# Zero products at the start, a norm turned on VectorE through DRAM, and new list priorities in a transformer layer

## The chip, the cores and the metric

One core of one Trainium2 chip runs the kernel. The metric is the device time of one execution in microseconds (us); the time given for a kernel is the median of several runs. The engines are called PE (TensorE, matmuls), ACT (ScalarE), DVE (VectorE), POOL (GpSimd) and SP (SyncE, which issues the DMAs here).

## The reference

A transformer layer on one sequence of S = 2048 rows and D = 640 columns, float32: layer norm, attention over eight keys at distances 0, 2, ..., 14, a residual, layer norm, a SwiGLU FFN with F = 1728, a residual. 32 heads of 20 columns.

```python
def _A_ref(x, wqkv, wo):
    qkv = (x @ wqkv).reshape(B, S, 3, H, Dh) ...
    off = jnp.arange(W) * dil            # W = 8, dil = 2
    idx = pos[:, None] - off[None, :]
    ...
    logits = jnp.einsum("bhsd,bhswd->bhsw", q, kg) * scale
    logits = jnp.where(mask[None, None, :, :], logits, -1e9)
    attn = _softmax(logits, axis=-1)
    o = jnp.einsum("bhsw,bhswd->bhsd", attn, vg)
    return o.transpose(0, 2, 1, 3).reshape(B, S, D) @ wo

def _B_ref(x, w_gate, w_up, w_down):
    return (_silu(x @ w_gate) * (x @ w_up)) @ w_down

h = x + _A_ref(_layernorm(x), A_wqkv, A_wo)
h2 = h + _B_ref(_layernorm(h), B_w_gate, B_w_up, B_w_down)
```

## The kernel before, in words

**Blocks.** The rows are cut into NB = 4 blocks of 512. A block lies on 128 partitions as NJ = 4 row tiles j of 640 columns. D is cut into NC = 5 chunks of 128.

**Products in three passes.** Every matmul operand is split into a high half, rounded to the type fp32r, and a low half, the remainder. A product is the sum of high x high, high x low and low x high. ACT makes the high half by a cast, DVE the low half by a subtraction. So each weight and each activation costs one ACT and one DVE instruction before PE may use both halves.

**First norm (ln1).** Rows are centred into the buffer XN; the factor 1/std is left for the eviction of the product (L405), so the products need only the centred rows. PE turns them into columns, four 128x128 transposes for each of five groups (x_columns, to_columns; L313), ACT casts them (L316), DVE subtracts (L317). Block 0 does so row tile by row tile (L361, L363, L364), with DVE computing the statistics of its first three tiles (L273 to L275). Blocks 0 and 2 go into the tile sha, blocks 1 and 3 into shb.

**Query, key, value (qkv, L400).** NG = 4 head groups of 8 heads; for each block, group and row tile 15 matmuls 128x480. Weights of a group are loaded in five pieces (load_wqkv; L374 and L376 split them). The results go to DRAM (ksc, vsc, qsc).

**Attention (att_load, att_qk, att_exp, att_av).** It runs on DVE, in 16 units of a block and a group, as long elementwise instructions and reductions (L448, L453, L479, L487; the first two take 2.8 us each), and ends with a turn (L494) and stores to osc.

**Output projection (wo, L569), residual, second norm, columns (ln2_columns).** wo(0) runs among the last qkv products, wo(b + 1) among the products of block b's FFN. Block 3 (TURN) makes its columns without PE: DVE turns 32x32 squares in place (L716), four transfers store them to xsc and one loads them back so that a chunk of columns lies on each partition (ln2_turn, L718 and L722); ACT and DVE then split them out of XN (L711, L712).

**FFN (ffn).** NF = 14 tiles of 128 columns of F. For each tile a gate and an up product into PSUM banks 5 and 6 (proj, L630: three passes of five matmuls for each bank), silu on ACT (L661), product on DVE (L662), split (L663, L665), and the down product of the tile before (down, L642), which accumulates in banks 0 to 4. Then finish adds the residual and stores (L681 to L700).

**The order of the work.** Nothing is issued in program order. Every step is first recorded with an engine, an estimated cost, the regions that it reads and writes, and a priority (Plan.add). Plan.order then runs a list scheduler over all engines: when an engine falls free, the ready operation with the lowest priority number goes next, and the list that results is the order in which each engine gets its instructions. SP transfers are given a modelled bus time and a latency (LAT, LAT0). PR holds the priorities. Products have priority 10, attention on DVE 20. One look-ahead rule exists: an operation of priority 20 or more waits if one of priority 1 would become ready before it ends. The list is fixed when the kernel is built; on the chip an engine waits for whatever its next instruction needs.

## Time and profile before

| | us |
|---|---|
| median of 3 runs | 869.96 (869.52 to 870.01) |
| the profiled execution | 870.27 |
| its span, first to last instruction | 868.5 |
| PE busy | 855.7 (99%) |
| DVE busy | 641.7 (74%) |
| ACT busy | 401.4 (46%) |
| POOL busy | 1.6 |

A row of the groups reads: line, engine, operation, tiles out<-in, shape, count, then busy time in us, mean ns of one, idle time of the engine just before them and what ended it. A row of the waits reads: engine and tile, line, what was waited for, then us in total, times, longest. A row of the windows reads: stretch, length, busy time of PE, weight loads (PEld), DVE, ACT and POOL with their counts, then the granted clock of PE, the DMA share and GB/s. The timeline merges neighbouring instructions of one line: start, length, engine, line, shape, count. The chain of waits is followed back from the last instruction; its rows are start, length, what. Matmuls are pipelined, so the time of a run of them divided by their number is the time that one costs, not the length of a single one.

### The profile page before, as it was taken

What the parts mean: (1) busy time and instruction counts of PE and PEld (TensorE: products, weight loads), DVE (VectorE), ACT (ScalarE), POOL (GpSimd) and SP (SyncE); (2) the same over time, 40 slices, a digit from 0 to 9 for tenths busy, and PEclk for the clock granted to TensorE, in tenths of its full rate; (3) what the DMA queues carried; (4) which work ended last, traced back from release to release, by engine and by line L of the source; (5) the groups of instructions that cost most, each with busy time, mean ns of one, the idle gap of its engine ahead of it and who ended that gap; (6) DMA issues with size and microseconds to landing.
All of it is one profiled execution on the core that took longest, in us unless ns stands there. A gap on an engine that the chain in (4) does not pass through costs nothing.

```text
span 868.5 us, 10718 instructions
## 1 busy us (share of the span) xinstructions
PE 855.7 (99%) x4036; PEld 726.8 (84%) x4036; DVE 641.7 (74%) x743; ACT 401.4 (46%) x651; POOL 1.6 (0%) x7
## 2 busy tenths in 40 slices
PE   6999999999999999999999999999999999999998
PEld 5888888889978888888888888878988888888886
DVE  6489699999999999999999999995212116333332
ACT  5857732223682434574443567443464334333321
POOL 0000000000000000000000000000000000000000
PEclk9999999999999999999999999999999999999999
DMA  7995764596887969659997986887437645322201
GB/s 252 272 292 162 202 174 133 155 289 173 296 243 236 295 227 272 191 158 305 363 300 237 304 228 194 237 304 244 141 124 246 243 148 181 107 91 91 97 26 61
DMA packets 74612, 180.11 MB, mean 207 GB/s; under 512 B 28720, under 2 KB 39344, under 8 KB 73792
## 3 DMA queue, kind: packets, MB, share of 16 engines
q1 hardware_dynamic: 74560, 179.43, 65.6%
q8 instruction: 31, 0.51, 0.3%
q14 instruction: 21, 0.17, 0.1%
HBM read 138.36 MB, written 41.03 MB: 207 GB/s over the span
## 4 chain that ended last, share of the span: by engine, by line
PE 77%; DVE 18%; issue 2%; DMA 2%; SPq 0%; ACT 0%; DVEq 0%
PE bank L630 32%; PE bank L400 23%; PE bank L642 16%; PE bank L569 5%; DVE fa L487 3%; DVE fa L479 3%; DVE fa L448 3%; DVE fa L453 3%; PE bank L313 1%; DVE acts L665 1%; DVE fa L662 1%; DMA osc<-fa 1%; DVE fa L494 1%; DVE shb L317 1%; DMA fa<-in_x_dram 1%
## 5 line engine op out<-in xcount | busy, mean ns | idle before, releaser
L630 PE MATMUL bank<-shb,ra 128*128 128x512 f32 x1620 | 381.2, 390 | 2.3 <-DVE shb L317 2.1
L630 PEld LDWEIGHTS bank<-shb,ra 128*128 128x128 f32 x1620 | 303.1, 188 | 66.2 <-DVE shb L317 3.3
L642 PE MATMUL bank<-ra,acts 128*128 128x512 f32 x656 | 160.3, 391 | 0.0
L642 PEld LDWEIGHTS bank<-ra,acts 128*128 128x128 f32 x656 | 122.5, 188 | 25.1
L662 DVE TENSOR_TENSOR fa<-bank,fa 128x512 f32<-128x512 f32 x52 | 35.7, 687 | 129.2 <-PE bank L630 128.9
L400 PE MATMUL bank<-ra,sha 128*128 128x480 f32 x480 | 108.4, 385 | 0.0
L400 PE MATMUL bank<-ra,shb 128*128 128x480 f32 x470 | 104.7, 380 | 0.0
L400 PEld LDWEIGHTS bank<-ra,sha 128*128 128x128 f32 x480 | 91.4, 192 | 13.7
L607 ACT CAST ra<-fa 128x1280 fp32r<-128x1280 f32 (+1 forms) x56 | 68.8, 1229 | 66.4 <-PE bank L630 64.7
L400 PEld LDWEIGHTS bank<-ra,shb 128*128 128x128 f32 x470 | 87.5, 188 | 12.8
L479 DVE TENSOR_TENSOR fa<-fa 128x1280 f32<-128x1280 f32 x64 | 93.7, 1487 | 1.0
L448 DVE TENSOR_TENSOR fa<-fa 128x2560 f32<-128x2560 f32 x32 | 90.3, 2821 | 2.6 <-DMA fa<-qsc 2.1
L487 DVE TENSOR_TENSOR fa<-fa 128x1280 f32<-128x1280 f32 (+2 forms) x96 | 89.7, 935 | 2.7
L453 DVE TENSOR_REDUCE fa<-fa 128x128 f32<-128x2560 f32 x32 | 90.1, 2815 | 0.6
L405 ACT ACTIVATE st<-bank,fa 128x480 f32<-128x480 f32 x64 | 42.0, 658 | 84.8 <-PE bank L400 82.0
L661 ACT ACTIVATE fa<-bank 128x512 f32<-128x512 f32 x52 | 31.1, 598 | 107.7 <-PE bank L630 107.6
L624 DVE TENSOR_TENSOR ra<-fa,ra 128x640 fp32r<-128x640 f32 (+1 forms) x82 | 64.7, 817 | 16.2 <-ACT ra L608 14.0
L569 PE MATMUL bank<-ra 128*128 128x320 f32 x480 | 74.5, 309 | 0.0
L569 PEld LDWEIGHTS bank<-ra 128*128 128x128 f32 x480 | 72.4, 188 | 2.1
L608 ACT CAST ra<-fa 128x640 fp32r<-128x640 f32 x56 | 40.7, 728 | 63.0 <-PE bank L642 62.8
L663 ACT CAST acts<-fa 128x512 fp32r<-128x512 f32 x52 | 32.3, 621 | 49.5 <-DVE fa L662 49.4
L642 PE MATMUL bank<-acts,ra 128*128 128x512 f32 x164 | 46.3, 390 | 0.1
(82 smaller groups left out, 486.1 us busy)
## 6 DMA issues: line engine op xcount, KB each, us to landing
fa<-in_ffn_dram SPq DMA_DIRECT2D x52, 960.0 KB, 6.0
ra<-lsc SPq DMA_DIRECT2D x26, 640.0 KB, 5.4
fa<-ksc SPq DMA_DIRECT2D x32, 440.0 KB, 5.8
fa<-vsc SPq DMA_DIRECT2D x32, 440.0 KB, 5.8
ra<-lsc SPq DMA_DIRECT2D x30, 320.0 KB, 3.7
lsc<-ra SPq DMA_DIRECT2D x13, 640.0 KB, 5.1
ksc<-st SPq DMA_DIRECT2D x32, 160.0 KB, 4.4
qsc<-st SPq DMA_DIRECT2D x16, 320.0 KB, 3.5
```

Source lines behind the costliest of these rows:

```text
L400: T.matmul(banks[bk][:, 0:480], l, r_(wq(g, w, c), 480), start=(p, c) == first_mm, stop=(p, c) == last_mm)
L405: P.add("ACT", act(480) + 0.06, lambda bk=bk, j=j: A.activation(stage_t()[:, so : so + 1920].rearrange("p (t j c) -> p t j c", t=3, j=NJ)[ ...
L448: P.add("DVE", dve(2560), lambda: V.tensor_tensor(f(PROD, 2560).rearrange("p (j w c) -> p j w c", j=2, w=W), window(ko, 2 * jp), f(qo + 32 ...
L453: P.add("DVE", dve(2560), lambda: V.tensor_reduce(f(lo + 128 * jp, 128), f(PROD, 2560).rearrange("p (n d) -> p n d", d=DH), axis=AX.X, op= ...
L479: V.tensor_tensor(f(PROD + 1280 * jj, 1280).rearrange("p (w h d) -> p w h d", w=W, d=DH), f(vo + 160 * j, 1280).rearrange("p (w h d) -> p ...
L487: V.tensor_add(dst(v), v[:, :, 0:m, :], v[:, :, m : 2 * m, :])
L569: T.matmul(banks[bk][:, 0:320], l, r_(m, 320), start=p == 0 and c == 0, stop=p == 2 and c == NC - 1)
L607: P.add("ACT", act(n), lambda: A.copy(r_(gu, n), f(raw, n)), r=[rf(raw, n)], w=[rr(gu, n)], prio=PR["fh"])
L624: P.add(eng, c, lambda o=o: E.tensor_sub(ra[p0:, lo + o : lo + o + 640], fa[p0:, raw + o : raw + o + 640], ra[p0:, hi + o : hi + o + 640]. ...
L630: T.matmul(banks[bk], r_(gu + 1280 * w + wid * c + col, 128), x2(a, c), start=p == 0 and c == 0, stop=p == 2 and c == NC - 1)
L642: T.matmul(banks[k], l, m, start=first and p == 0, stop=last and p == len(passes) - 1)
L662: P.add("DVE", dve(512), lambda so=so: V.tensor_mul(f(so, 512), banks[6], f(so, 512)), r=[pb(6), rf(so, 512)], w=[rf(so, 512)], prio=0)
```

## The change

Five things change.

1. POOL clears 128 columns of the weight tile (WARM). PE multiplies them with themselves 20 times ahead of everything else, into bank 4, and three times more behind the transposes of block 0's first row tile. The results are overwritten.
2. Block 3's first norm (TURN1) is turned as its second one was: ACT centres the rows into XN sorted for DVE's turn, using the source as scratch space; one DVE turn of 2560 columns, four stores to a new DRAM tile ysc, one load, then five casts on ACT and five subtractions on DVE out of XN. The 20 PE transposes of that norm are gone. The code of ln2_turn becomes turn_rows and serves both norms.
3. In the first FFN tile of each block the up product's pass high x high comes before the gate product's second pass. Other tiles keep their order.
4. The look-ahead rule takes priorities up to 1 instead of exactly 1, and PE holds a product back for at most 0.3 us if an operation with wo(0)'s priority is about to be ready.
5. 19 of the 22 priorities in PR have other values (x, ost and fl stay), and there is a new one for the stores of item 2.

```diff
+TURN1 = (3,)
-PR = {'x': 6, 'wqd': 2.5, 'wqh': 3, 'wql': 2.5, 'qev': 1, 'kvs': 3, 'atl': 3, 'exp': 8, 'ost': 0.5, 'wod': 6, 'woh': 3, 'wol': 2, 'old': 1, 'fld': 3, 'lst': 3, 'wev': 1, 'fh': 2, 'fl': 8, 'ln1': 6, 't1': 2, 'wo0': 1.5, 'wo': 2}
+PR = {'x': 6, 'yst': 1, 'wqd': 8, 'wqh': 2.2, 'wql': 2.2, 'qev': 0.5, 'kvs': 6, 'atl': 2.2, 'exp': 1.2, 'ost': 0.5, 'wod': 1.5, 'woh': 0.9, 'wol': 1.5, 'old': 0.9, 'fld': 1, 'lst': 6, 'wev': 1.5, 'fh': 1.2, 'fl': 8, 'ln1': 3, 't1': 4, 'wo0': 0.4, 'wo': 4}
...
             prio, n = ready[e][0]
+            if e == "PE" and prio >= 10:
+                soon = min((a for a, m in pend[e] if ops[m][4] == PR["wo0"]), default=1e9)
+                if soon < t + 0.3:
+                    free[e] = soon
+                    continue
             if prio >= 20:
-                soon = min((a for a, m in pend[e] if ops[m][4] == 1), default=1e9)
+                soon = min((a for a, m in pend[e] if ops[m][4] <= 1), default=1e9)
                 if soon < t + ops[n][1] - 0.3:
                     free[e] = soon
                     continue
...
+                inplace = self.center and self.turned
...
+                if inplace:
+                    def rows():
+                        A.activation(src(j), src(j), AF.Identity, accum_out=f(SUM, 1))
+                        A.mul(f(NEG, 1), f(SUM, 1), -1.0 / D)
+                        A.activation(self.sorted_row(j), src(j).rearrange("p (f t) -> p f t", t=32), AF.Identity, bias=f(NEG, 1))
+                    P.add("ACT", 1.95, rows, ..., prio=self.prio)
+                    P.add("ACT", 1.0, lambda: A.activation(src(j), src(j), AF.Square, bias=f(NEG, 1), accum_out=f(SS, 1)), ..., prio=self.prio + 1)
+                    return
...
+        def turn_rows(scratch, key, b, prio, sprio):
+            P.add("DVE", dve(2560), lambda: V.transpose(f(XN, 2560), f(XN, 2560)), ..., prio=prio)
+            for q in range(4):
+                P.add("SP", 0.65, lambda q=q: Q.dma_start(
+                    scratch[b, :, q, :].rearrange("(f c) t -> c f t", c=32),
+                    fa[32 * q : 32 * q + 32, XN : XN + 2560].rearrange("p (f t) -> p f t", f=20)), ..., prio=sprio, nbytes=nb(640, 512))
+            P.add("SP", 0.65, lambda: Q.dma_start(f(XN, 2560).rearrange("p (k t) -> p k t", k=NC), scratch[b].rearrange("(k c) q t -> c k (q t)", c=128)), ..., prio=sprio, nbytes=nb(640, 2048))
+
+        def turned_columns(t, nm, prio):
+            for k in range(NC):
...
+                w = lambda a, k=k: [(nm, 2560 * a + 640 * j + 128 * k, 2560 * a + 640 * j + 128 * k + 128) for j in range(NJ)]
+                P.add("ACT", act(512), lambda col=col, src=src: A.copy(col(0), src()), ..., w=w(0), prio=prio)
+                P.add("DVE", dve(512), lambda col=col, src=src: V.tensor_sub(col(1), src(), col(0).bitcast(F32)), ..., w=w(1), prio=prio)
...
+        WARM = XH + 1280
+
+        def warm(n, after=()):
+            def mm():
+                for _ in range(n):
+                    T.matmul(banks[4][:, 0:128], r_(WARM, 128), r_(WARM, 128), start=True, stop=True)
+            P.add("PE", 0.2 * n, mm, r=[rr(WARM, 128), *after], w=[pb(4)], prio=0)
...
+                if b in TURN1:
+                    turn_rows(ysc, "Y", b, PR["ln1"], PR["yst"])
+                    turned_columns(t, nm, PR["t1"])
+                    return
...
             for j in range(NJ):
+                if j == 1:
+                    warm(3, [("b5", 0, 0.25)])
...
-        def proj(bk, gu, col, wid):
+        def proj(bks, gu, wid, first):
+            passes = ((0, 0), (0, 1), (1, 0))
...
+            todo = [(n, p) for n in range(len(bks)) for p in range(3)]
+            if first:
+                todo.insert(1, todo.pop(3))
+            for n, p in todo:
+                w, a = passes[p]
+                P.add("PE", 1.145, lambda ...: mm(bk, 128 * n, p, w, a), ..., w=[pb(bks[n])], prio=10)
...
+        P.add("POOL", 0.3, lambda: G.memset(r_(WARM, 128).bitcast(F32), 0.0), w=[rr(WARM, 128)], prio=0)
         load_x(0, (0,))
+        warm(20)
```

More of the change, by code (lines that the diff above doesn't have):

```diff
@@ L177, in program @@
         xsc = dr.tile([NB, D, 4, 128], F32, name="xsc")
+        ysc = dr.tile([NB, D, 4, 128], F32, name="ysc")
         lsc = dr.tile([NF, 128, 1920], F32, name="lsc")
@@ L251, in one @@
                 SUM, NEG, SS = self.SUM + j, self.NEG + j, self.SS + j
-                junk = (lambda: act_t()[:, 3072:3712]) if self.turned else (lambda: f(xo, 640))
+                inplace = self.center and self.turned
+                junk = (lambda: src(j)) if inplace else (lambda: act_t()[:, 3072:3712]) if self.turned else (lambda: f(xo, 640))
+                if inplace:
[3 more added lines that the diff above has]
+                        A.activation(self.sorted_row(j), src(j).rearrange("p (f t) -> p f t", t=32), AF.Identity, bias=f(NEG, 1))
+                    P.add("ACT", 1.95, rows, r=[self.srcr(j)], w=[self.srcr(j), rf(XN, 2560), rf(SUM, 1), rf(NEG, 1)], prio=self.prio)
+                    P.add("ACT", 1.0, lambda: A.activation(src(j), src(j), AF.Square, bias=f(NEG, 1), accum_out=f(SS, 1)),
+                          r=[self.srcr(j), rf(NEG, 1)], w=[self.srcr(j), rf(SS, 1)], prio=self.prio + 1)
+                    return
                 def s1():
@@ L264, in one, with sorted_row @@
                           r=[rf(xo, 640)], w=[self.srcr(j), rf(SS, 1)], prio=self.prio + 1)
+            def sorted_row(self, j):
+                return f(XN, 2560).rearrange("p (f j t) -> p f j t", j=NJ, t=32)[:, :, j, :]
             def one_dve(self, j):
@@ L300, in apply @@
                 if self.turned:
-                    o = f(XN, 2560).rearrange("p (f j t) -> p f j t", j=NJ, t=32)[:, :, j, :]
+                    o = self.sorted_row(j)
                     i = lambda j: self.src(j).rearrange("p (f t) -> p f t", t=32)
@@ L304, in apply @@
                       r=[self.srcr(j), rf(self.NB + j, 1), rf(self.RS + j, 1)], w=[rf(XN, 2560) if self.turned else rf(xo, 640)], prio=self.prio)
+        def turn_rows(scratch, key, b, prio, sprio):
+            P.add("DVE", dve(2560), lambda: V.transpose(f(XN, 2560), f(XN, 2560)), r=[rf(XN, 2560)], w=[rf(XN, 2560)], prio=prio)
+            for q in range(4):
+                P.add("SP", 0.65, lambda q=q: Q.dma_start(
+                    scratch[b, :, q, :].rearrange("(f c) t -> c f t", c=32),
+                    fa[32 * q : 32 * q + 32, XN : XN + 2560].rearrange("p (f t) -> p f t", f=20)),
+                    r=[rf(XN, 2560)], w=[(f"{key}{b}", q, q + 1)], prio=sprio, nbytes=nb(640, 512))
+            P.add("SP", 0.65, lambda: Q.dma_start(f(XN, 2560).rearrange("p (k t) -> p k t", k=NC), scratch[b].rearrange("(k c) q t -> c k (q t)", c=128)),
+                  r=[(f"{key}{b}", 0, 4)], w=[rf(XN, 2560)], prio=sprio, nbytes=nb(640, 2048))
+        def turned_columns(t, nm, prio):
+            for k in range(NC):
+                col = lambda a, k=k: t()[:, 2560 * a : 2560 * a + 2560].rearrange("p (j c q t) -> p c j q t", j=NJ, c=NC, q=4)[:, k]
+                src = lambda k=k: f(XN + 512 * k, 512).rearrange("p (q j t) -> p j q t", q=4, j=NJ)
+                w = lambda a, k=k: [(nm, 2560 * a + 640 * j + 128 * k, 2560 * a + 640 * j + 128 * k + 128) for j in range(NJ)]
+                P.add("ACT", act(512), lambda col=col, src=src: A.copy(col(0), src()), r=[rf(XN + 512 * k, 512)], w=w(0), prio=prio)
+                P.add("DVE", dve(512), lambda col=col, src=src: V.tensor_sub(col(1), src(), col(0).bitcast(F32)),
+                      r=[rf(XN + 512 * k, 512)] + w(0), w=w(1), prio=prio)
         def x_columns(dst, dstr, prio):
@@ L340, in ln1 @@
             srcr = lambda j: rf(XR + 640 * j, 640)
-            st = LnStats(b, src, srcr, 1 if b == 0 else PR["ln1"], rs=RS1 + 4 * b, center=True)
+            st = LnStats(b, src, srcr, 1 if b == 0 else PR["ln1"], rs=RS1 + 4 * b, center=True, turned=b in TURN1)
             if b:
@@ L625, in split, with mm @@
                       r=[rf(raw + o, 640), rr(hi + o, 640)], w=[rr(lo + o, 640)], prio=PR["fl"])
-        def proj(bk, gu, col, wid):
-            def mm(p, w, a):
+        def proj(bks, gu, wid, first):
+            passes = ((0, 0), (0, 1), (1, 0))
+            def mm(bk, col, p, w, a):
                 for c in range(NC):
                     T.matmul(banks[bk], r_(gu + 1280 * w + wid * c + col, 128), x2(a, c), start=p == 0 and c == 0, stop=p == 2 and c == NC - 1)
-            for p, (w, a) in enumerate(((0, 0), (0, 1), (1, 0))):
-                P.add("PE", 1.145, lambda p=p, w=w, a=a: mm(p, w, a), r=[rr(gu + 1280 * w, wid * NC), ("shb", 2560 * a, 2560 * a + 2560)], w=[pb(bk)], prio=10)
+            todo = [(n, p) for n in range(len(bks)) for p in range(3)]
[3 more added lines that the diff above has]
+                w, a = passes[p]
+                P.add("PE", 1.145, lambda bk=bks[n], n=n, p=p, w=w, a=a: mm(bk, 128 * n, p, w, a), r=[rr(gu + 1280 * w, wid * NC), ("shb", 2560 * a, 2560 * a + 2560)], w=[pb(bks[n])], prio=10)
         def down(i, ao, dn, k):
@@ L658, in ffn @@
                 if i < NF - 1:
-                    proj(5, gu, 0, 256)
-                    proj(6, gu, 128, 256)
+                    proj((5, 6), gu, 256, i == 0)
                     P.add("ACT", act(512), lambda so=so: A.activation(f(so, 512), banks[5], AF.Silu), r=[pb(5)], w=[rf(so, 512)], prio=0, table="silu")
@@ L667, in ffn @@
                 else:
-                    proj(5, gu, 0, 128)
+                    proj((5,), gu, 128, False)
                     P.add("ACT", act(512), lambda so=so: A.activation(fa[64:128, so : so + 512], banks[5][0:64, :], AF.Silu), r=[pb(5)], w=[rf(so, 512)], prio=0, table="silu")
@@ L707, in ln2_columns @@
                 return
-            for k in range(NC):
-                col = lambda a, k=k: shb[:, 2560 * a : 2560 * a + 2560].rearrange("p (j c q t) -> p c j q t", j=NJ, c=NC, q=4)[:, k]
-                src = lambda k=k: f(XN + 512 * k, 512).rearrange("p (q j t) -> p j q t", q=4, j=NJ)
-                P.add("ACT", act(512), lambda col=col, src=src: A.copy(col(0), src()), r=[rf(XN + 512 * k, 512)], w=[hi(k)], prio=prio)
-                P.add("DVE", dve(512), lambda col=col, src=src: V.tensor_sub(col(1), src(), col(0).bitcast(F32)),
-                      r=[rf(XN + 512 * k, 512), hi(k)], w=[lo(k)], prio=prio)
-        def ln2_turn(b, prio):
-            P.add("DVE", dve(2560), lambda: V.transpose(f(XN, 2560), f(XN, 2560)), r=[rf(XN, 2560)], w=[rf(XN, 2560)], prio=prio)
-            for q in range(4):
-                P.add("SP", 0.65, lambda q=q: Q.dma_start(
-                    xsc[b, :, q, :].rearrange("(f c) t -> c f t", c=32),
-                    fa[32 * q : 32 * q + 32, XN : XN + 2560].rearrange("p (f t) -> p f t", f=20)),
-                    r=[rf(XN, 2560)], w=[(f"X{b}", q, q + 1)], prio=PR["ost"], nbytes=nb(640, 512))
-            P.add("SP", 0.65, lambda: Q.dma_start(f(XN, 2560).rearrange("p (k t) -> p k t", k=NC), xsc[b].rearrange("(k c) q t -> c k (q t)", c=128)),
-                  r=[(f"X{b}", 0, 4)], w=[rf(XN, 2560)], prio=PR["ost"], nbytes=nb(640, 2048))
+            turned_columns(lambda: shb, "shb", prio)
+        P.add("POOL", 0.3, lambda: G.memset(r_(WARM, 128).bitcast(F32), 0.0), w=[rr(WARM, 128)], prio=0)
         load_x(0, (0,))
+        warm(20)
         P.add("SP", 0.45, lambda: Q.dma_start(f(MASK, 160), const_in), w=[rf(MASK, 160)], prio=0, nbytes=nb(128, 640))
@@ L760, in program @@
                 if b + 1 in TURN:
-                    ln2_turn(b + 1, PR["wo"])
+                    turn_rows(xsc, "X", b + 1, PR["wo"], PR["ost"])
             do_down = ffn(b)
```

## The prediction

> **What bounds the kernel now.** I read the engine shares and the waits first, then windows of 20 us, then the chain and the timelines of the places where those windows are not full.

> ```profile
> span 868.5 us, 10718 instructions
> PE 855.7 (99%) x4036; PEld 726.8 (84%) x4036; DVE 641.7 (74%) x743; ACT 401.4 (46%) x651; POOL 1.6 (0%) x7
> PE bank L361 <- DVE fa L275: 6.6, 2, 5.5
> PE bank L630 <- DVE shb L317: 2.1, 2, 1.4
> 0.00:20.00 20.00, 13.43 (x56) 11.43 (x57) 14.07 (x39) 10.78 (x25) 0.21 (x4) 1.00 0.72 238
> ...
> 240.00:260.00 20.00, 18.33 (x87) 14.16 (x86) 19.72 (x25) 15.79 (x23) 0.10 (x1) 1.00 0.82 250
> ...
> 860.00:880.00 20.00, 4.65 (x23) 3.51 (x21) 3.42 (x6) 0.30 (x1) 0.00 (x0) 0.91 0.18 66
> ```

> TensorE (PE) is the bound: 868.5 - 855.7 = 12.8 us idle. Of this 6.6 lie in the first 20 us (two waits for L275, the first until 5.5), 20.00 - 18.33 = 1.7 in 240 to 260, and 8.5 - 4.65 = 3.85 behind the last matmul; of the two waits of L630 the longer, 1.4, is in 240 to 260, and the other, 2.1 - 1.4 = 0.7, stands at the next block's border. So an edit pays only by taking work off PE, by speeding PE up, or by closing one of these holes. VectorE (DVE) is as full while attention runs (19.72 of 20 in 240 to 260).

> The chain and PE's timeline show a second loss that counts as busy:

> ```profile
> 7.90 1.33 PE bank L361 x5
> 9.22 6.48 PE bank L400 x20
> ...
> 17.66 14.29 PE bank L400 x66
> ...
> 46.28 0.87 PE bank L313 x8
> ...
> 266.72 6.80 PE bank L630 x30
> ```
> ```profile
> 15.54 0.71 PE L361 MATMUL bank<-fa 128*128 128x128 f32 x5
> 8.88 4.75 PE L400 MATMUL bank<-ra,sha 128*128 128x480 f32 x11
> 13.42 2.06 PE L400 MATMUL bank<-ra,sha 128*128 128x480 f32 x8
> ```

> Five transposes take 1.33 us at 7.90 and 0.71 at 15.54; eleven products take 4.75 us from 8.88 and eight take 2.06 from 13.42. PE thus starts at about half speed and changes near 13.6, though the granted clock reads 1.00 in that window. On the path: 20 products at 6.48 / 20 = 0.324 us against 14.29 / 66 = 0.2165 cost 20 x 0.1075 = 2.15 us too much, the second five transposes 1.33 - 0.71 = 0.62.

> **The change, part by part.** The sum stands against the profiled execution's 870.27 us (span 868.5 and 1.77 around it); the median shown, 869.96, is 0.31 lower, which I subtract at the end.

> A, *block 3's first norm.* Twenty transposes leave PE: 8 take 0.87 us in the chain, so 20 x 0.109 = **-2.2 us**. In exchange:

> ```profile
> L716 DVE STREAM_TRANSPOSE fa<-fa 128x2560 f32<-128x2560 f32 x1 | 2.8, 2846 | 0.1
> xsc<-fa SPq DMA_DIRECT2D x4, 320.0 KB, 6.4
> fa<-xsc SPq DMA_DIRECT2D x1, 1280.0 KB, 7.0
> qsc<-st SPq DMA_DIRECT2D x16, 320.0 KB, 3.5
> 96.91 0.83 ACT L258 ACTIVATE fa<-fa 128x640 f32<-128x640 f32 x1
> 122.80 13.12 PE L400 MATMUL bank<-ra,sha 128*128 128x480 f32 x60
> ```

> DVE gets one more turn of 2.85 us, and SP's queue five transfers of the kind that block 3's second norm already makes; the five casts on ScalarE (ACT) and five subtractions on DVE stay, with SBUF as their source instead of PSUM. The centred rows are ready at 96.91 + 0.83 = 97.7. Turn, store and load follow: 97.7 + 2.85 + 6.4 + 7.0 = 114, and with one 2.8 us attention instruction ahead of the turn 117. The columns write shb for all four row tiles at once, so they must wait for block 1's last products anyway; block 2's 60 products, 122.80 to 135.9, stand between that and the first reader. Five subtractions behind attention pieces fit into 13 us. Hidden here; without that cover the trip's 16 us would stand on PE. The DVE's 2.85 us push attention back and are paid from its own slack (below).
> [...]

> B, *zero products.* Twenty 128-wide products ahead of everything, three more behind the first transposes. No row shows them. The memset that they wait for can hardly end before DVE's first one does, so I put their begin at about 1.0.

> ```profile
> 0.81 0.06 DVE L220 MEMSET fa<- 128x1 f32 x1 [0.81 <-PEq L806]
> 7.76 0.65 DVE L376 TENSOR_TENSOR ra<-fa,ra 128x480 fp32r<-128x480 f32 x1
> ...
> 14.46 0.65 DVE L376 TENSOR_TENSOR ra<-fa,ra 128x480 fp32r<-128x480 f32 x1
> ```

> One costs at least 128 / 480 of the slow L400 product (4.75 / 11 = 0.43 with its start, so 0.12) and at most that whole product; the nearest row is the slow transpose of the same 128x128 shape, at most 1.33 / 5 = 0.27. I take 0.21: the twenty end near 5.3, just before the first transposes. At the upper end they would end near 9.6 and delay PE by 4 us. If PE is at full speed when the second transposes start at 7.90, 0.62 + 2.15 = 2.8 us are saved. Not quite all: the weights' low halves come from DVE in four L376 from 7.76 + 0.65 = 8.4 to 15.1, and a faster PE meets them sooner; I charge 0.5. **-2.3 us**, bounds -2.8 and +4.
> [...]

> C, *the two orderings around the FFN's first tile.* At 241 to 251:

> ```profile
> 241.29 2.83 DVE L448 TENSOR_TENSOR fa<-fa 128x2560 f32<-128x2560 f32 x1
> ...
> 244.94 1.88 DVE L317 TENSOR_TENSOR shb<-bank,shb 128x512 fp32r<-128x512 f32 x3
> 246.74 2.81 DVE L453 TENSOR_REDUCE fa<-fa 128x128 f32<-128x2560 f32 x1
> 249.46 1.28 DVE L317 TENSOR_TENSOR shb<-bank,shb 128x512 fp32r<-128x512 f32 x2
> ```
> ```profile
> 247.05 1.74 PE L630 MATMUL bank<-shb,ra 128*128 128x512 f32 x5
> 250.20 2.01 PE L630 MATMUL bank<-shb,ra 128*128 128x512 f32 x6 [1.40 <-DVE shb L317]
> ```

> PE's gate pass on the high halves (L630 x5) ends at 248.8 and the next waits for the last low halves, which stand behind L453. Between 247.05 and 250.20 PE does 5 x 6.80 / 30 = 1.1 us of work in 3.15, so 2.0 us are lost. The change (first=True in proj) puts the up pass on high halves, another 1.1 us, into that hole, and the planner's rule now holds attention pieces (prio 20) back for any operation of prio 0 to 1, and wo of block 0 is now 0.4 instead of 1.5. That can take L448 (2.83) and L453 (2.81) out of the norm's chain. But PE will also arrive 2.2 + 2.3 = 4.5 us earlier by A and B, so those 5.6 us are needed to move the norm's chain along. I take **-1.5 us** here; bounds +4.5 (A and B given back) and -2.0. At the next border the other wait of L630 goes: **-0.7**. Of the border after that no wait is listed: 0.

> D, *the new priorities* reorder every engine's list. The present list leaves 1.7 + 0.7 = 2.4 us of holes inside the run. A new one can't have fewer than none and may have several; I charge **+1.5 us**, bounds 0 and 5 (twice the present holes). Start (5.5) and tail (3.85) stay.

> Sum: -2.2 - 2.3 - 1.5 - 0.7 + 1.5 = -5.2; 870.27 - 5.2 - 0.31 = 864.76. **Forecast 864.8 us.**

> **The rivals.** R1, *the zero products don't open the clock.* The stretch from 5.3 to 7.9 holds only transposes, three products and a pause; if transposes don't count as work for the clock, the twenty products alone (4.2 us) seldom fill what the trace shows is needed, 4.7 us of L400 products, and the clock opens after real products as now. Then B is 0: 864.8 + 2.3 = 867.1. [...]

> R2, *the norm's chain at 241 to 251 eats the early gain.* PE comes 4.5 us earlier, the chain does not: DVE is full, and 2.85 us fuller. For it: PE already waits for DVE exactly there, and 240 to 260 is the one window in the middle of the run that is not full. Against it: the 5.6 us of attention pieces that the rule can move out. Then only the up pass's 1.1 and the 0.7 remain: 869.96 - 1.8 + 0.8 (half of D) = 869.0.

> R3, *slower: held-back attention.* The rule now also keeps DVE idle ahead of the FFN's own products (prio 0).

> ```profile
> L494 DVE STREAM_TRANSPOSE fa<-fa x3: 511/511/512, 440.2 to 469.9; 128x320 f32<-128x320 f32 x3
> L303 ACT ACTIVATE fa<-h,fa x4: 906/914/925, 532.1 to 535.4; 128x640 f32<-128x640 f32 x4
> 560.79 1.08 ACT L316 CAST shb<-bank 128x512 fp32r<-128x512 f32 x2
> ```

> Place: the end of block 1's FFN. Block 2's attention ends at 469.9, its norm at 536.3, its columns are wanted at 560.8: 24.5 us of slack. L662 is known to the planner one 1.145 us matmul pass plus 0.2 us ahead, so each tile before 469.9 (13 of block 0's FFN and some five of block 1's) can hold DVE up to 1.35 us, and L665 behind it up to 0.8 more (the cast between them and 0.2): 18 x 2.15 = 39 us. Beyond 24.5 PE starves: 14 us, which gives 878.8. It decides from 1.4 us a tile; slower than before begins at a stall of 871.7 - 864.8 = 6.9. Against it: L665 becomes known only when ACT starts, when DVE has usually gone on.

> R4, *the trip through DRAM is late.* Should the load stand in SP's queue as block 3's second one may, 6 us later than PE needs it, the time is about 870.8.

> **How the numbers follow.** Forecast 0.61, R1 0.15, R2 0.08, R3 0.12, R4 0.04. About 0.2% (1.7 us) is what a measurement of this kernel can tell from no change, so faster ends at 868.2. The forecast's case and R1 lie below it, and a part of R2's spread: faster 0.78. R2's rest and R4: same 0.10. R3: slower 0.12. The lower end: all terms at their best give -2.2 - 2.8 - 2.0 - 0.7 = -7.7, 862.3; with 0.1 for the spread I take 862.2. The upper end takes in R1 and R2: 869.5, leaving out R3 and R4.

> **What would show it.** A: L313 x100 instead of x120, a second DVE turn of 2560 columns, and block 3's products without a wait. B: the second five L361 in about 0.7 us and L400 at 0.217 from the first on; a 0.43 there is R1. C: PE idle in 240 to 260 under 1 us, and L453 not between the L317. R2 is right if that window is emptier than 18.33. R3 is right if DVE's share in 260 to 470 falls below 9 tenths and PE waits near 560. The forecast is wrong if PE's idle time, less start and tail, is above 5 us.

## Result and the profile after

The changed kernel takes 863.54 us (median of 6 runs, 862.56 to 867.86) against 869.99 for the kernel before beside it (6 runs, 869.41 to 871.01): ratio 0.9931, 95% interval [0.991, 0.9953]. The profiled execution is the shortest of the six, 862.56, so its gain of 7.7 us is more than the median's 6.45. What follows explains the profiled gain.

Page, waits of PE and windows (their figures: length of the window; busy time of PE, PE's weight load, DVE, ACT, POOL; granted clock, DMA share, GB/s) of the changed kernel; L368 are the zero products, L456 is the old L400, L688 the old L630, L417 the old L361, L353 and L357 the old L313 and L317:

```profile
span 860.8 us, 10726 instructions
PE 855.2 (99%) x4039; PEld 728.7 (85%) x4039; DVE 645.2 (75%) x744; ACT 404.4 (47%) x652; POOL 1.8 (0%) x8
```
```profile
PE bank L368 <- POOL ra L772: 1.0, 1, 1.0
PE bank L688 <- ACT shb L356: 0.6, 1, 0.6
```
```profile
0.00:20.00 20.00, 18.94 (x87) 17.12 (x88) 14.86 (x42) 12.62 (x30) 0.42 (x5) 1.00 0.81 272
240.00:260.00 20.00, 19.44 (x89) 15.97 (x88) 18.16 (x19) 12.84 (x16) 0.10 (x1) 1.00 1.01 345
```

PE's busy time hardly differs from before (855.2 and 855.7), but the 23 zero products are in it (20 in 4.53 us, 3 in 0.88, below). Of the waits for L317 none is left; 0.56 us of idle time remain at the border near 242 us. To see where the 7.7 us came from, I took the start of the same PE instruction in both traces:

| PE instruction | before | after | difference |
|---|---|---|---|
| second five transposes of block 0 | 7.90 | 7.32 | -0.6 |
| 21st qkv product | 16.01 | 14.22 | -1.8 |
| 61st qkv product | 25.31 | 23.51 | -1.8 |
| 481st (block 2's first) | 122.80 | 119.14 | -3.65 |
| block 0's FFN, 17th product | 253.18 | 247.16 | -6.0 |
| block 1's FFN, 101st | 437.89 | 431.81 | -6.1 |
| block 2's FFN, 17th | 572.47 | 564.81 | -7.65 |
| end of the last matmul | 864.65 | 857.06 | -7.6 |
| span | 868.5 | 860.8 | -7.7 |

So there are four places: the start (-1.8), block 3's transposes (-1.85), the border of the first FFN (-2.4) and that of the third (-1.55). The start, from PE's timeline of the changed kernel:

```profile
1.00 4.53 PE L368 MATMUL bank<-ra 128*128 128x128 f32 x20 [1.00 <-POOL ra L772]
5.59 1.33 PE L417 MATMUL bank<-fa 128*128 128x128 f32 x5
6.57 0.88 PE L368 MATMUL bank<-ra 128*128 128x128 f32 x3
7.32 1.33 PE L417 MATMUL bank<-fa 128*128 128x128 f32 x5
8.30 5.62 PE L456 MATMUL bank<-ra,sha 128*128 128x480 f32 x20
13.76 0.71 PE L417 MATMUL bank<-fa 128*128 128x128 f32 x5
```

The twenty products fill 1.00 to 5.3 without a pause. Still the transposes at 5.59 and 7.32 take 1.33 us, the slow figure, and 20 products of L456 take 5.62 us where full speed needs about 4.5 (23 of them take 5.14 at 119.14): the change to full speed comes at 10.6 us, more than 3 us after the last zero product.

The border near 242 us, DVE and PE:

```profile
241.98 0.68 DVE L357 TENSOR_TENSOR shb<-bank,shb 128x512 fp32r<-128x512 f32 x1
...
243.60 0.69 DVE L357 TENSOR_TENSOR shb<-bank,shb 128x512 fp32r<-128x512 f32 x1 [0.94 <-ACT shb L356]
...
244.21 2.81 DVE L509 TENSOR_REDUCE fa<-fa 128x128 f32<-128x2560 f32 x1
```
```profile
242.59 0.47 PE L688 MATMUL bank<-shb,ra 128*128 128x512 f32 x1
243.62 4.61 PE L688 MATMUL bank<-shb,ra 128*128 128x512 f32 x19 [0.56 <-ACT shb L356]
```

L509 is the old L453, which stood between the L317. Now DVE waits idle for the last cast (0.94) and takes the attention piece behind the last low half. PE then runs 19 products without a wait.

The border near 568 us of the kernel before, DVE and PE (timelines from 556 to 574), and the same place in the changed kernel (550 to 567):

```profile
569.33 0.68 DVE L317 TENSOR_TENSOR shb<-bank,shb 128x512 fp32r<-128x512 f32 x1
570.06 4.16 PE L630 MATMUL bank<-shb,ra 128*128 128x512 f32 x17 [0.65 <-DVE shb L317]
```
```profile
557.38 1.99 DVE L357 TENSOR_TENSOR shb<-bank,shb 128x512 fp32r<-128x512 f32 x3
561.15 6.09 PE L688 MATMUL bank<-shb,ra 128*128 128x512 f32 x26
```

Before, the last low half came at 569.33, behind the residual's additions (L692, L696), when the FFN's first products had run from 567.77 on. Now all five are made before the first product.

Block 3's first norm in the changed kernel, from DVE's timeline, from the instructions on the tile ysc (smallest, median and largest time in ns, first and last start), and from ACT's timeline:

```profile
92.99 2.83 DVE L328 STREAM_TRANSPOSE fa<-fa 128x2560 f32<-128x2560 f32 x1
```
```profile
L330 SPq DMA_DIRECT2D ysc<-fa x4: 325/629/2062, 95.8 to 98.9; - x4
...
L334 SPq DMA_DIRECT2D fa<-ysc x1: 537/537/537, 111.1 to 111.1; - x1
```
```profile
121.64 2.69 ACT L342 CAST shb<-fa 128x512 fp32r<-128x512 f32 x5
```

The load back is issued at 111.1, 12 us behind the last store: the stores took 4.5 us (median) to land, and for the rest it stood behind other transfers in SP's queue (eleven were issued between the last store and it). It landed at 119.8. PE does not notice, since block 2's products run from 119.14 and no wait of PE on L342 or L343 is listed.

### The profile page after: what moved, and what is told of

Its sections match the earlier page's. It is cut to its first block, busy times and chain, and to the rows that moved or that the text cites. A ratio compares the mean times of both kernels' runs of the same rounds, so it can differ in the third digit from the quotient of the medians.

```text
span 860.8 us, 10726 instructions
## 1 busy us (share of the span) xinstructions
PE 855.2 (99%) x4039; PEld 728.7 (85%) x4039; DVE 645.2 (75%) x744; ACT 404.4 (47%) x652; POOL 1.8 (0%) x8
## 4 chain that ended last, share of the span: by engine, by line
PE 93%; DMA 4%; DVE 2%; ACT 0%; issue 0%; DVEq 0%; ACTq 0%
PE bank L688 43%; PE bank L704 21%; PE bank L456 19%; PE bank L625 8%; DMA fa<-qsc 1%; DMA qsc<-st 1%; DMA fa<-in_wo_dram 1%; PE bank L353 1%; DVE fa L535 1%; PE bank L417 0%; DMA fa<-in_x_dram 0%; DVE fa L543 0%; DVE fa L504 0%; DVE fa L509 0%; PE bank L746 0%
## 5 line engine op out<-in xcount | busy, mean ns | idle before, releaser
L688 PE MATMUL bank<-shb,ra 128*128 128x512 f32 x1620 | 379.4, 390 | 0.6 <-ACT shb L356 0.6
L688 PEld LDWEIGHTS bank<-shb,ra 128*128 128x128 f32 x1620 | 303.1, 188 | 62.9 <-ACT shb L356 0.9
L723 DVE TENSOR_TENSOR fa<-bank,fa 128x512 f32<-128x512 f32 x52 | 35.9, 689 | 123.6 <-PE bank L688 114.3
L456 PE MATMUL bank<-ra,sha 128*128 128x480 f32 x480 | 107.5, 382 | 0.0
L456 PE MATMUL bank<-ra,shb 128*128 128x480 f32 x470 | 103.1, 379 | 0.0
L456 PEld LDWEIGHTS bank<-ra,sha 128*128 128x128 f32 x480 | 90.3, 190 | 13.4
L456 PEld LDWEIGHTS bank<-ra,shb 128*128 128x128 f32 x470 | 87.9, 188 | 13.1
L509 DVE TENSOR_REDUCE fa<-fa 128x128 f32<-128x2560 f32 x32 | 90.0, 2813 | 0.4
L680 DVE TENSOR_TENSOR ra<-fa,ra 128x640 fp32r<-128x640 f32 (+1 forms) x82 | 64.5, 818 | 13.6 <-ACT ra L664 13.6
```

Source lines behind the costliest of these rows:

```text
L456: T.matmul(banks[bk][:, 0:480], l, r_(wq(g, w, c), 480), start=(p, c) == first_mm, stop=(p, c) == last_mm)
L509: P.add("DVE", dve(2560), lambda: V.tensor_reduce(f(lo + 128 * jp, 128), f(PROD, 2560).rearrange("p (n d) -> p n d", d=DH), axis=AX.X, op= ...
L680: P.add(eng, c, lambda o=o: E.tensor_sub(ra[p0:, lo + o : lo + o + 640], fa[p0:, raw + o : raw + o + 640], ra[p0:, hi + o : hi + o + 640]. ...
L688: T.matmul(banks[bk], r_(gu + 1280 * w + wid * c + col, 128), x2(a, c), start=p == 0 and c == 0, stop=p == 2 and c == NC - 1)
```

## Experiments

Each was timed against the kernel before on the same chip. Ratios are to that kernel.

### The changed kernel again, without zero products, and with wide ones

a1_again is the changed kernel unaltered. e1_no_products leaves out the 23 products:

```diff
-                for _ in range(n):
+                for _ in range(0):
```

e2_wide_products issues fewer and wider ones:

```diff
-                for _ in range(n):
-                    T.matmul(banks[4][:, 0:128], r_(WARM, 128), r_(WARM, 128), start=True, stop=True)
+                for _ in range(10 if n == 20 else 1):
+                    T.matmul(banks[4], r_(WARM, 128), r_(WARM, 512), start=True, stop=True)
```

> The changed kernel once more, on one chip with the next three, for a second sample of its start. Theory 1 (the zero products shorten PE's slow start): L456 changes from 0.40 to 0.217 us a product near 10.5 us again or earlier, the time is 863.5. Theory 2 (the moment of the change is chance): it falls anywhere from 7.3 to 13.8, and the time scatters by half of that, 1.5 us either way.

> The changed kernel without the 23 zero products; every other instruction in the same order. Theory 1: the speed changes near 13.5 us as in the kernel before, so PE's 20th product of L456 comes 1.2 to 1.8 us later, and the whole time is later by as much: 864.7 to 865.3. Theory 2: no difference beyond scatter, 863.5. Theory 3 (a norm's chain on VectorE sets when the first FFN starts, and early time is lost there): the 20th product is 1.2 to 1.8 us later, the first FFN product is not, 863.5.

> The changed kernel with 512-wide zero products, ten at first and one behind the first transposes, instead of 20 and 3 of 128; all else in the same order. A 128-wide product took 0.213 us at the slow speed where a quarter of a 0.427 us product of 512 would take 0.107, so it keeps the array busy for half of the time. Theory 1a (busy time of the array is what counts): the speed changes before the second transposes at 7.3, and half of the 3.1 us from there to 10.45 is saved: 862.0. Theory 1b (any product counts): the change stays near 10.5 us, 863.5. Theory 2: chance, 862 to 865.

| | median us (range) | ratio, interval | full speed from | 21st qkv product |
|---|---|---|---|---|
| a1_again | 865.47 (861.57 to 867.42) | 0.995 [0.9931, 0.9968] | 10.9 | 14.34 |
| e1_no_products | 863.01 (862.65 to 865.96) | 0.9932 [0.992, 0.9944] | 10.7 | 14.24 |
| e2_wide_products | 862.00 (861.41 to 862.74) | 0.9914 [0.9901, 0.9926] | 4.3 | 12.96 |

PE's timeline without products, and with wide ones:

```profile
5.49 1.33 PE L417 MATMUL bank<-fa 128*128 128x128 f32 x5 [5.49 <-DVE fa L295]
7.31 1.33 PE L417 MATMUL bank<-fa 128*128 128x128 f32 x5 [0.49 <-DVE fa L295]
8.29 5.66 PE L456 MATMUL bank<-ra,sha 128*128 128x480 f32 x20
```
```profile
1.32 3.92 PE L368 MATMUL bank<-ra 128*128 128x512 f32 x10 [1.32 <-POOL ra L772]
5.57 0.77 PE L417 MATMUL bank<-fa 128*128 128x128 f32 x5 [0.33 <-DVE fa L295]
```

Without any product the start is the same as with 23 narrow ones: 8.29 and 5.66 against 8.30 and 5.62. In these profiles the narrow products do nothing that can be measured, and in the medians neither. Ten wide ones bring full speed during themselves (4.3 us), and the first transposes take 0.77 instead of 1.33. Over all kernels of this study full speed came at 9.0, 9.2, 10.3, 10.6, 10.9, 10.9 and 13.5 us with narrow products, at 10.7, 11.8 and 13.8 with none, at 4.3, 4.7, 6.0 and 7.0 with wide ones.

What decides the moment can be read from the traces, which keep the time of every change of the granted clock. In every run the time between two changes is a whole number of steps of 3.413 us: 1 step for the drop in e7 below, 69 steps (235.52 us) ahead of the drop in e4, 249 steps (849.92 us) in the changed kernel. So the changes fall on a grid of that step, and the grid stands differently against the start in each run. Single steps, with PE's busy time in them, show what counts:

| step, us | what PE did in it | at its end |
|---|---|---|
| e3, 2.15 to 5.56 | narrow products, busy for 3.37 of 3.41 | half speed stays |
| e11, 2.34 to 5.75 | narrow products, then 0.2 us of transposes, busy for 3.40 | half speed stays |
| e10, 1.30 to 4.71 | wide products, busy for 3.39 | full speed |
| e7, 0.15 to 3.56 | wide products from 1.32 on, busy for 2.24 | half speed stays |

By its busy time PE is equally busy in the first three, so the width of the products makes the difference, as theory 1a has it. Theory 1a's reason for it fits: at half speed ten wide products took 4.63 us (e7) and twenty narrow ones, with half as many columns in all, 4.53 (the changed kernel), so by this estimate the array stands still for half of the time between narrow ones. The narrow products may still help to fill a pause: in e3 and e11 the steps that brought full speed (at 9.0 and 9.2) held transposes, the last three narrow products and only 0.7 and 1.0 us of L456. No run tests that by itself.

The grid also gives the spread (theory 2), and the gain at the start. In the kernel before, the changed one and e1 it stands nearly alike, with steps that end at 10.36, 10.55 and 10.67 us. In the kernel before, PE is busy for 2.46 us of that step, and half speed lasts for one step more, to 13.8. In the other two the second transposes come 0.6 us earlier, PE is busy for 3.41 and 3.36 us, and full speed comes. That is one execution of each; with the grid elsewhere the difference can be another.

The changed kernel's own scatter (861.57 to 867.42 here) has a place too. Waits of PE in a1_again, and the DVE instruction that stands before them:

```profile
PE bank L353 <- DVE sha L357: 0.6, 1, 0.6
PE bank L353 <- DVE shb L357: 0.6, 1, 0.6
...
PE bank L353 <- ACT fa L275: 0.5, 1, 0.5
```
```profile
44.54 2.83 DVE L504 TENSOR_TENSOR fa<-fa 128x2560 f32<-128x2560 f32 x1 [7.13 <-DMA fa<-qsc]
```

These waits, at 50 to 78 us, are absent or short in the profile above. The first norms' transposes of blocks 1 and 2 stand in PE's list behind low halves that DVE makes late after a load from qsc came late. They account for the profiled difference: 863.1 against 860.8 in span, of which 2.2 us arise between 40 and 78 us. In the changed kernel's first profile the same instruction waited 4.96 us for its load, here 7.13. In e2 such waits take back 1.4 us of what its start gains, so that its profiled span is 861.0.

### Block 3's transposes: back with a new list, and back as dead work

e3_pe_turn sets `TURN1 = ()`. e11_dead_transposes keeps the whole list and adds 20 transposes of the identity into a free bank, planned at no cost:

```diff
+ [P.add("PE", 0.0, lambda: [T.transpose(banks[7][:, 128 * q : 128 * q + 128], ident, ident) for q in range(4)], r=[rf(IDENT, 128)], w=[pb(7)], prio=10) for u in range(5)]
```

> The changed kernel with block 3's first norm turned on PE as before (TURN1 empty); the list is made anew with the new priorities. Theory 1 (each transpose taken off PE is worth its 0.109 us, all hidden in DVE's and the DMA's cover): 20 of them back, 863.5 + 1.9 to 2.2 = 865.4 to 865.7. Rival (the time is set by DVE's chain at 242 us or by the new list, and the transposes lay beside it): 863.5 or less.

> The changed kernel with 20 extra transposes on PE, of the identity into a free bank, just ahead of block 3's first products; every other instruction in the same order. It gives back PE's work of the old norm and nothing else. Theory 1 (PE's own work is on the path there): 20 x 0.109 = 2.2 us more than the changed kernel, 865.0 to 865.7. Theory 2 (the wait near 242 us takes it up): 863.5, at most 0.8 more.

e3: 868.95 us (865.39 to 874.14), ratio 0.9997 [0.9979, 1.0015]: 5.4 us above the changed kernel's first measurement and 3.5 above a1_again on the same chip, not 2.2. In its profile 2.2 us are lost at the third FFN's border, where the changed kernel has no wait. e11: 867.53 us (864.81 to 868.09), ratio 0.9962 [0.9947, 0.9976]. In e11's profiled execution the 481st qkv product starts 1.66 us later than in the changed kernel's (waits at 57 and 75 us, as in a1_again), the 721st 3.84 later, the end of the last matmul 3.79. Between the first two marks lie the 20 transposes: 3.84 - 1.66 = 2.18 us, which is 20 x 0.109, and all of it is there at the end. So PE's own work counts in full in the changed kernel's list. e11's median, 867.53, lies above the ranges of both theories; in its profile the two waits ahead of the transposes, which cost 2.4 us, account for that. What e3 lost beyond 2.2 us fits its new list, but its executions scatter over 9 us and only one was profiled.

### Priorities, rule and up pass

e4_old_prio puts the old values of PR back (yst 1 kept). e5_old_rule takes the rules back:

```diff
-                if soon < t + 0.3:
+                if soon < t - 1e9:
...
-                soon = min((a for a, m in pend[e] if ops[m][4] <= 1), default=1e9)
+                soon = min((a for a, m in pend[e] if ops[m][4] == 1), default=1e9)
```

e6_no_first leaves the up pass in its old place (`if first:` becomes `if False:`). e8_turn_only has the old priorities, the old rules, no products and no up pass, so it is the kernel before with the new turn alone.

> The changed kernel with the old priorities PR (yst 1 kept), made into a list anew; products, turn, look-ahead rules and up pass stay. Theory 1 (the gains at the FFN borders near 242 and 562 us, 2.4 and 1.5, come from the priorities, above all wo0, which the rule then covers): both come back, 863.5 + 3.9 = 867.4. Theory 2 (they come from the rules and the up pass): 863.5. Theory 3 (a list tuned for this very kernel avoids waits anywhere): a new list has holes in other places too, above 868, with a wide scatter.

> The changed kernel with the old look-ahead (priority exactly 1, PE never held), list made anew; new priorities, products, turn and up pass stay. Theory 1 (the rule keeps 2.8 us attention pieces out of the norm's chain near 242 us): that border loses 1 to 2.5 us again, 864.5 to 866. Theory 2 (priorities alone do it): 863.5. Theory 3 (any other list is worse): above 866, holes elsewhere.

> The changed kernel without the up pass ahead of the gate's second pass; the list is nearly the same. Theory 1 (the up pass fills the wait for the low halves, as predicted): 1.1 us lost near 242 and up to 1 us near 562, 865 to 865.6. Theory 2 (the low halves now come before the gate's first pass ends, since no attention piece stands between them): no wait is left to fill, 863.5.

> The kernel before with block 3's first norm turned on VectorE through DRAM and nothing else (old priorities, old rule, no products, no up pass); the list is made anew. Theory 1 (a transpose off PE is worth its 0.109 us in any list): 870.0 - 2.2 = 867.8. Theory 2 (a list with priorities not chosen for it has waits of its own, as with the old priorities and with the old rule at 871.3): 868.5 to 873, and the 2.2 us can't be seen in the time.

| | median us (range) | ratio, interval |
|---|---|---|
| e4_old_prio | 871.33 (870.47 to 873.77) | 1.0012 [1.0003, 1.0021] |
| e5_old_rule | 871.34 (870.33 to 872.77) | 1.0017 [1.0009, 1.0026] |
| e6_no_first | 862.74 (862.07 to 863.36) | 0.9914 [0.9901, 0.9928] |
| e8_turn_only | 871.54 (870.82 to 872.10) | 1.0016 [1.0007, 1.0025] |

In the lists tried, neither the priorities nor the rules gain anything without the other, and the turn alone is 0.16% slower than no turn, as theory 2 of e8 had it. Waits of PE in e4, e8 and e5:

```profile
PE bank L353 <- DVE shb L357: 3.7, 1, 3.7
...
PE bank L688 <- DVE shb L357: 0.9, 1, 0.9
```
```profile
...
PE bank L353 <- DVE shb L357: 3.7, 1, 3.7
PE bank L454 <- ACT st L459: 0.8, 1, 0.8
```
```profile
PE bank L688 <- DVE shb L357: 1.9, 2, 1.0
PE bank L456 <- ACT ra L449: 1.4, 1, 1.4
```

With the old priorities and the turn, PE waits 3.7 us near 244 for a low half, whether or not rules, products and up pass are there. With the new priorities and the old rule, the same products start later than in the changed kernel: PE loses 3.1 us up to the first FFN's border, 2.9 more at the second's and 2.1 more at the third's. Theory 1 of e4 and of e5 had the place right and the size too small; theory 3 describes both results.

The up pass is worth nothing here (862.74 without). The next experiment shows why.

### Early time in the kernel before, and the clock at the border

e7_before_wide is the kernel before with the wide zero products alone; e9_before_wide_first has the up pass too. Both keep the old list but for a few lines.

> The kernel before with ten 512-wide zero products at first and one behind the first transposes, same order otherwise. Both theories: full speed from about 4.5 us, the 20th product of block 0 near 13 instead of 16 us. Theory 1 (the chain of wo and norm on VectorE sets the first FFN product at 247, early time is lost there): 869.6, no change. Theory 2 (early time is kept): 2.5 to 3 us less, 866.6 to 867.

> The kernel before with the wide zero products and with the up pass ahead of the gate's second pass; the list is otherwise nearly that of the kernel before. Theory 1 (PE's clock fell to half at 249.3 for 3.4 us in the run with wide products alone because PE idled for 1.5 of 3.0 us at that border; the up pass fills 1.1 us of it): the clock stays up, the up pass and the border at 568 give 1.1 and up to 0.8, so 867.7 - 1.9 = 865.8 in nearly all executions instead of 867.7 or 869.2. Theory 2 (as in the changed kernel without the up pass, it fills no wait): 867.7 to 869.2, in two groups again.

e7: 869.13 us, ratio 0.9983 [0.9975, 0.9992]. Its eleven times lie in two groups, 867.69 to 867.83 (three) and 869.00 to 869.68 (eight). In its profiled execution (869.38) the 21st qkv product comes 2.6 us earlier than before, the first FFN product too (244.48 against 247.05): the early time is kept up to there, so theory 1 is wrong. Behind that border only 0.9 of the 2.6 us are left. Windows of e7 behind the wait, with PE's granted clock as the third figure from the end:

```profile
246.00:249.00 3.00, 1.51 (x6) 0.86 (x5) 3.00 (x5) 2.68 (x4) 0.00 (x0) 1.00 0.93 271
249.00:252.00 3.00, 3.00 (x9) 2.38 (x8) 2.96 (x5) 0.44 (x1) 0.00 (x0) 0.55 0.98 393
252.00:255.00 3.00, 3.00 (x13) 2.38 (x13) 2.83 (x2) 2.37 (x4) 0.10 (x1) 0.88 1.00 282
```

PE is busy for 1.51 of 3 us, and then the clock is at half for 3.4 us (249.3 to 252.7). Half speed for 3.4 us costs 1.7, which is all that is lost there. The same happened in e9 (3.4 us from 248.4) and, behind a wait of 3.7 us, in e8 (3.4 us from 247.3) and e4, there for 6.8 us:

```profile
246.00:249.00 3.00, 0.46 (x4) 0.42 (x4) 2.86 (x10) 2.52 (x4) 0.00 (x0) 1.00 1.02 244
249.00:252.00 3.00, 2.64 (x9) 1.85 (x9) 3.00 (x6) 2.98 (x5) 0.00 (x0) 0.51 0.99 328
252.00:255.00 3.00, 3.00 (x7) 1.83 (x7) 2.97 (x6) 0.51 (x2) 0.10 (x1) 0.50 1.06 416
```

In the profiled executions of the kernel before and of the changed kernel it did not happen, though the kernel before has the same wait of 1.40 us as e7. The grid of 3.413 us is a likely reason: in e7 the whole wait lies in one step (245.91 to 249.32, PE busy for 1.92 us), in the kernel before it is shared by two (busy for 2.74 and 2.41). PE's busy time alone does not decide, though: in e11 the step from 74.02 to 77.43, with a wait of 2.0 us, had PE busy for 1.60 us, and the clock stayed up. e7's two groups, 1.4 us apart, fit a drop in some executions and none in others, but only one execution of each was profiled.

e9: 869.52 us (867.90 to 870.98), ratio 0.9991 [0.9982, 1.0]; not 865.8, but near theory 2, though its eleven times form no two groups. Its border, from PE's timeline:

```profile
243.12 1.25 PE L313 MATMUL bank<-fa 128*128 128x128 f32 x8
244.50 1.75 PE L643 MATMUL bank<-shb,ra 128*128 128x512 f32 x5
248.24 8.03 PE L643 MATMUL bank<-shb,ra 128*128 128x512 f32 x27 [1.99 <-DVE shb L317]
```

The up pass stands next in PE's list behind the five products, needs only high halves, and still waits for L317. The code tells what for: it writes bank 6, and x_columns puts its fifth group of transposes into bank 6 as well. The bank is free only when DVE has made the fifth low half, the last of the five that the gate's second pass waits for. So the up pass can't start before the wait that it was to fill is over. In the changed kernel there is no such wait left, and it is not needed.

### Wide products without the up pass

e10_wide_no_first is the changed kernel with wide products and without the up pass.

> The changed kernel with wide zero products and without the up pass. Wide products: full speed from 4.3 to 7.0 us as in the two kernels with them, 862.0. If width is not what opens the clock: near 10.5 us, 863. The up pass: worth nothing in this list, so no more than 0.3 us from the kernel with both.

862.32 us (860.93 to 863.05), ratio 0.9909 [0.9896, 0.9923]; full speed from 4.7 us. With e2 (0.9914 [0.9901, 0.9926]) that makes two kernels with wide products that beat the kernel before by 0.9%; on e2's chip the changed kernel stood at 0.995 [0.9931, 0.9968], outside e2's interval. Against the changed kernel's first measurement, [0.991, 0.9953], and against the kernel without products, [0.992, 0.9944], the intervals overlap.

## The prediction, step by step

**The forecast** of 864.8 us was 1.3 us above the measured 863.54. That it came so near is in part luck. The profiled execution gained 7.7 us where the sum has 5.2: A and B together gained 0.85 us less than forecast, C 1.75 more, and the 1.5 us charged in D did not arise. The median lies nearer because the other executions are longer. On a second chip the same kernel took 865.47 (a1_again, 869.56 for the kernel before).

**A, right.** Forecast -2.2, in the profile -1.85 between the marks, and 2.18 in e11, where nothing else differs. The cover was as argued, though the trip ended later than the 117 us of the prediction: the load left at 111.1, landed at 119.8, and the casts ran at 121.6, still ahead of block 3's products. So a load held up in SP's queue, as in R4, did occur, but not later than PE needed it. A store of 320 KB to ysc landed in 4.5 us (median of four), and the load of 1280 KB in 8.7, where the prediction's sum has 6.4 and 7.0.

**B, right in size, wrong in cause.** Forecast -2.3, measured -1.8 at the 21st product. The step that failed is "if PE is at full speed when the second transposes start at 7.90": it was an assumption that no row of the kernel before showed, and with narrow products full speed came at 9.0 us at the earliest (e3); e1 has the same start without any. R1's claim about the products was true, though no run tests by itself its condition, that transposes don't count as work for the clock, and 4.7 us of L400 products were not needed: full speed came after 2.25 us of them in the changed kernel (8.30 to 10.55) and 2.4 in e1. Its price was not right: 0.6 of the 1.8 came from the earlier second transposes, which e1 has too, and the rest from the clock, which came up at 10.6 instead of 13.8 us, one step of its grid earlier, in e1 as well. My working of their cost was exact (20 in 4.3 us from 1.0 on) and beside the point. Narrow products kept PE busy for 3.37 and 3.40 us of a step of 3.41 in e3 and e11 without effect; wide ones, busy for 3.39 of the step from 1.30 to 4.71 in e10, brought full speed at its end.

**C, right in place, too small, and again by another path.** Forecast -1.5 and -0.7, measured -2.4 and -1.55. The term "the up pass fills 1.1 us" was wrong: bank 6 was overlooked (e6, e9). What removed the waits is the order of DVE's list, for which priorities and rule are both needed (e4, e5). The other listed wait of 0.7 stands at the border near 568, not at the next block's as the prediction has it; at that one, near 408, nothing changed. Near 568 more was won than the wait: 0.5 us ahead of the first product and 0.95 behind it, of which 0.65 are the listed wait.

**D, mis-sized.** I charged 1.5 us for new holes. In the profiled execution the new list has fewer holes than the old one; the holes that it has, at 50 to 78 us, come and go (a1_again, e11). They probably are what separates the median from the profiled run, about 1 us; that is not shown, since only one of those six executions was profiled.

**The rivals.** R2 is wrong as stated: e7's early time arrives at the border whole, since the norm's chain moves along with it, and what takes 1.65 of the 2.6 us is a drop of the clock. R3 ran part of its way. Block 2's last attention turns (L550, the old L494) and its norm (L323, the old L303), each by its line, and the first cast of its columns, from ACT's timeline:

```profile
L550 DVE STREAM_TRANSPOSE fa<-fa x2: 511/512/512, 479.0 to 485.8; 128x320 f32<-128x320 f32 x2
```
```profile
L323 ACT ACTIVATE fa<-h,fa x4: 913/920/926, 546.3 to 550.4; 128x640 f32<-128x640 f32 x4
```
```profile
554.61 1.08 ACT L356 CAST shb<-bank 128x512 fp32r<-128x512 f32 x2
```

Block 2's attention ends 16 us later than before (485.8 against 469.9), its norm 15 us later, and 3.3 of the 24.5 us of slack are left before the columns. A fifth more would have used them up. The prediction's sign for it, a DVE share below 9 tenths, is clear in one window only (10.21 of 20 us in 420 to 440; 17.84 in 400 to 420). DVE's waits for PE ahead of L723 (the old L662), which are of the kind that R3 means, come to 9.0 us between 260 and 490 (eleven, the longest 1.5; in the kernel before 1.7 in four, between 260 and 475). The emptiest window comes mostly from other waits, 3.7 us for a load from ksc and 3.5 for a cast of weights on ACT, which R3 did not have.

**What decided.** The gain is 1.85 us of PE work, about 4 us at two borders that, in the lists tried, only the new priorities and the new rule together win, and 1.8 us at the start that the zero products did not bring.

## What to carry to other kernels

In a list fixed at build time an edit's worth is that of the list that comes out: taking the transposes off PE was worth 2.2 us in the changed kernel's list, and the same turn alone made the kernel 1.4 us slower. So test an edit as dead work in an unchanged list, where its own price shows, before remaking the list. Of the products meant to bring up the clock only the wide ones did here (full speed at 4.3 to 7.0 us, against 9.0 to 13.5 with narrow ones and 10.7 to 13.8 with none); and when filling a wait with other work, look at which bank that work writes and who has yet to read it.

## What the runs showed of the hardware

PE's clock fell to half for 3.4 us after PE was busy for 1.51 of 3 us with a wait of 1.4 us (e7), and for 3.4 and 6.8 us after a wait of 3.7 us (e8, e4). In e7 the step ahead of the drop was busy for 1.92 of 3.41 us, while in e11 the clock stayed up after one that was busy for 1.60. What is counted stays open. The granted clock in the windows showed this drop (0.55, 0.51), but read 1.00 throughout the slow start.
